# Attention with a softplus feed-forward on one core: low query parts turned by a DMA, their shifts by TensorE and small DMAs, and a planner with other DMA lags

## The chip, the cores and the metric

One core of a Trainium2 chip runs one launch of the kernel. The metric is device time in microseconds (us), lower is better. An execution is timed as a whole; one execution was also profiled.

## The reference

```python
q_pool = q.reshape(B, H, S // 2, 2, D).mean(axis=3)          # B 4, H 8, S 1152, D 64
scores = 1 / sqrt(D) * q_pool @ k.transpose(0, 1, 3, 2)
scores = scores - scores.max(axis=-1, keepdims=True)
attn = exp(scores) / (exp(scores).sum(axis=-1, keepdims=True) + 1e-9)
x = (attn @ v).transpose(0, 2, 1, 3).reshape(B * 576, H * D) # 2304 x 512
h = x @ w_in                                                 # w_in 512 x 2048
out = softplus(h) @ w_out                                    # w_out 2048 x 512
```

Neighbouring queries are averaged in pairs, so 576 query rows meet 1152 keys. q, k, v and w_in are drawn eight times larger than usual, so scores are large and the row maximum is needed to high precision.

## The kernel before

**Units of work.** The 32 heads go in 16 pairs (u0 to u15), two heads on one set of tiles. Attention of a pair is 18 steps: 9 key tiles for the first 256 query columns, then 9 for the other 320. Batches give 8 feed-forward blocks (U0 to U7, w_in and softplus; D0 to D7, w_out), which `ORDER` (L445) weaves between later pairs.

**Precision.** An fp32 operand is split into two fp16 parts, high and low, scaled by a power of two. Keys become `kcat` (high beside low) and queries `qcat` (high twice); both are turned into `kT` and `qA`, by TensorE for pair 0 and by a DMA transpose for the others (L736, L763). Scores are one matmul of `kT` with `qA` and a second one of `kB` (high keys plus two rows of a constant) with `qB`. `qB` holds the low queries (64 rows) and two rows of shift, the negated row maximum as a high and a low fp16 number.

**Preparing a pair** (`prepare`, L629). Load k and q, add neighbouring queries (L685), sums of squares on ScalarE (L686, L687), one matmul that adds both over partitions and a chain of small VectorE operations that makes both scales at once (`scale_from_squares`, L369), then the splits. The low queries go to `qlow` (L756).

**The maxima** (`maxima`, L797). For each of the 9 query tiles, TensorE scores high queries against key differences `kD` and keys, ScalarE takes the relu of one (L818), VectorE joins them and keeps the maximum (L822), and L838 does so for the last keys. A reduction (L857) and two small operations (L352, L355) put the shift as two more columns into `qlow`. TensorE turns `qlow`, low queries and shift together, against an identity (L879, L882: 20 matmuls for a pair), and ScalarE or VectorE copies the result to `qB` in three pieces (L896, L899).

**Attention** (`attention`, L930). Scores (L363), exp on ScalarE (L958), product with v (L967). The sums of exp are added up over key tiles by GpSimd or VectorE (`acc`, L435), and TensorE adds over partitions (L1038); for pairs in `SUMMED` (0, 2 and 4) TensorE does all of it (L983). Then a reciprocal by way of three small DMAs (L1054 to L1061) and a product.

**What sets the order.** `Sched` (L98) is a planner that runs while the program is built: each step has one or more engines it can go to, a price there, and a priority; tables `NUDGE` and `LEAN` shift priorities and prices. What it plans becomes the fixed order of instructions on each engine, and the engines then wait for each other by semaphores. DMAs are issued by one queue, SyncE's (SP), in the planned order. `LAG` (L103) is what it believes to pass from the end of a step to the start of one that depends on it; to a DMA 1,250 to 1,400 ns. Ring buffers (`raw` 4, `p` 4, `qlow` 2, PSUM `m` 3 and `s` 2) hold steps back.

Of the kernel before, what the change touches and what calls it, by code (L numbers as in the profile page):

```python
# [8 lines left out]
F32 = mybir.dt.float32  # L9
# [12 lines left out]
    "prep": [-1.5, 0, 3.75, 1, -3.25, 18.5, -0.75, 0, 0, -23.5, 26, 6.75, 0.25, 3, 6.75, 8.75],  # L22
    "value": [-7, 0, 6, -6.75, -3.25, 0, 4.75, -21.75, 10, -7.5, 5.25, -19, 0, -4.25, -8.75, -4.5],
    "most": [7.5, 3.75, 1, 0, -7.75, -2.25, 7.25, 9.25, 10, 9, 10.5, 0, 0, 21.75, 0, 0],
    "shift": [5.75, -3, -19.75, 17.75, -18.25, 12.5, -9.5, 0.5, -4, -19.75, 2.25, 2.25, 0, 1.25, 0, 8.5],
    "attend": [0.75, -2.25, -1, -8.5, 0, -34, -13.5, -10.25, 4.25, 0, 8.25, -4.5, 0, 6, 3, -2.25],
    "product": [-3.5, -0.5, 10, -6.25, 11.5, 9.25, 0, -1, 8, 24.75, 5.75, 1.75, 1, 6.5, 7.25, 0],
    "close": [12.5, -1.5, -29.5, -7.75, 14.75, -14.5, -4.25, 20.25, -13.5, -12, -1.25, 0, 0, 0.25, 14.75,
        -5.75],
    "win": [4.5, 9.5, 5.5, -20.25, 0, -9.75, -3.75, -48],  # L30
    "wout": [-0.5, -9, -18.5, 17.5, 39.25, -40.25, 12.25, 2.25, -1.5, -18.5, -11.25, -4.75, -1.25, 0, 26.25,
        4.75],
    "wparts": [0, -1, -7, 8.25, 3.75, -3.25, 42, -6.25, 19, -21, 0, -20.5, -17.5, -7.5, 2.5, 4.25],
    "split": [-26.75, -1.25, -1.75, 8.75, -4.75, 17.75, 1, 14],
    "up": [16.25, 1.5, 3, -3.25, 5.25, -23.25, -14.5, 2.75],
    "down": [1.75, -3, 37.25, -5.25, 4, -0.25, -4.25, 3.25],
# [16 lines left out]
        "split": [-100, -2200, 0, -1950, 1150, 0, 250, -200],
        "up": [1050, 400, -150, 0, 850, -100, -2300, 100],
        "down": [0, 0, 100, -1350, 50, 1800, -50, 650],
    },
    "ACT": {
        "prep": [500, 200, -3350, 0, -50, -750, -0, -1500, 250, 1300, 1850, -150, -800, 0, 0, 250],
        "value": [-350, 50, -1150, 150, 0, 0, -2050, 1000, -1200, -200, 400, 800, -650, 2750, -350, 900],
        "most": [100, -1400, 0, -0, -950, 100, 0, 0, -50, -1100, -350, 0, 600, -800, 0, 0],  # L60
        "shift": [-650, -400, 0, 100, -1400, -1350, -700, -900, 500, 2500, -4650, -900, -2150, 0, 900, 800],
        "attend": [1650, -1000, 2200, 500, -400, 1400, -250, 0, -100, 0, 350, 400, 0, 0, -0, 0],
        "product": [800, -1950, -2050, 3250, 900, 150, 1400, -3850, 2450, 1700, 1700, 100, 1100, 400, -150,
            1550],
        "close": [-450, -500, -1900, -900, -100, 1250, 0, 150, 800, 150, 0, 450, -1750, -1350, 750, 1250],
        "win": [950, -3550, -550, 100, 0, 300, -1750, -650],
        "wout": [300, 900, -750, -350, -550, 0, -1650, 50, 50, 150, 2900, 1050, -400, -700, 0, 100],
        "wparts": [1500, -250, 50, 0, 3300, 350, 3450, 2400, -400, -500, -1900, 0, 0, -400, 2600, 250],
        "split": [100, 0, -2250, -600, -1050, -400, -250, -200],
        "up": [-600, 2400, 50, 1500, -1750, 650, 600, 0],  # L70
        "down": [0, -2150, -900, 3150, 100, -900, 400, 900],
# [26 lines left out]
class Sched:  # L98

    LAG = {  # L103
        "PE": {"DVE": 200.0, "ACT": 200.0, "PE": 0.0, "DMA": 1300.0},
        "DVE": {"DVE": 40.0, "ACT": 45.0, "POOL": 60.0, "PE": 55.0, "DMA": 1400.0},
        "ACT": {"DVE": 45.0, "ACT": 40.0, "POOL": 60.0, "PE": 55.0, "DMA": 1250.0},
        "POOL": {"DVE": 50.0, "ACT": 60.0, "POOL": 50.0, "PE": 60.0, "DMA": 1300.0},
# [142 lines left out]
def pool1(n):  # L250
    return 145.0 + n * 0.95
# [1008 lines left out]
```

## Time and profile before

| what | value |
|---|---|
| time, median of 3 runs (lowest, highest) | 853.09 us (852.1, 857.29) |
| the profiled execution | 852.98 us |
| its span, first to last instruction | 851.3 us |
| TensorE busy, share of the span | 804.3 us, 94% |
| VectorE, ScalarE, GpSimd busy | 539.0, 492.8, 317.5 us |
| mean granted TensorE clock | 0.989 |

The trace's engines are PE (TensorE matmuls), PEld (its weight loads), DVE (VectorE), ACT (ScalarE), POOL (GpSimd) and SP (the queue that issues DMAs). A matmul's busy time has its pipeline in it, so a busy PE can still wait inside.

### The profile page before, as it was taken

Reading aid. Unit: us, or ns where it says so; the run is one execution under the profiler, and the core shown is the slowest. Engines: PE = TensorE matmul, PEld = TensorE weight load, DVE = VectorE, ACT = ScalarE, POOL = GpSimd, SP = SyncE. Lnnn points to the kernel's source line nnn. Section 1 sums busy time; section 2 is a strip of 40 time slices with the busy share of each in tenths; the row PEclk is TensorE's granted clock in tenths of the full one; section 3 lists DMA queues with packets and bytes.
Section 4 is the critical chain, followed back from the end, with each engine's and each line's share of the span. In section 5 each row is a group of like instructions: output and inputs, shape, how many; then the busy total and the mean of one; then the engine's idle time right before and its main releaser. Section 6 shows DMA issues by size and latency. Waiting matters only on the chain.

```text
span 851.3 us, 24268 instructions
## 1 busy us (share of the span) xinstructions
PE 804.3 (94%) x10250; PEld 579.0 (68%) x10250; DVE 539.0 (63%) x1171; ACT 492.8 (58%) x823; POOL 317.5 (37%) x272
## 2 busy tenths in 40 slices
PE   3898898989899999999999999999999999999997
PEld 2465566558767688768666787667876678775754
DVE  7778888889998876675685643466556626012520
ACT  4788899889897427562665545457865572120210
POOL 0105418521249201331676514611268882090000
PEclk9899999999999999999999999999999999999999
DMA  8718657358664710411652330420603000000000
GB/s 306 163 36 215 146 169 203 114 127 186 173 134 139 120 54 2 125 28 46 125 78 79 90 79 13 83 89 19 94 13 92 22 15 10 22 15 25 2 14 25
DMA packets 98093, 74.23 MB, mean 87 GB/s; under 512 B 64960, under 2 KB 79296, under 8 KB 97984
## 3 DMA queue, kind: packets, MB, share of 16 engines
q1 hardware_dynamic: 97984, 72.68, 34.6%
q8 instruction: 80, 1.31, 0.7%
q14 instruction: 29, 0.24, 0.1%
HBM read 49.81 MB, written 4.79 MB: 64 GB/s over the span
## 4 chain that ended last, share of the span: by engine, by line
PE 69%; DVE 11%; ACT 6%; DMA 5%; POOL 5%; issue 3%; SPq 1%; ACTq 0%; DVEq 0%; POOLq 0%
PE s L363 30%; PE m L363 26%; PE pv L967 12%; POOL acc L435 3%; DMA kT<-kcat 2%; ACT p L958 2%; PE pv L983 2%; DMA raw<-in_k_dram 1%; ACT raw L523 1%; DVE w L355 1%; DVE qlow L355 1%; DVE kcat L355 1%; DVE g L822 1%; PE m L1038 1%; DVE acc L435 1%
## 5 line engine op out<-in xcount | busy, mean ns | idle before, releaser
L958 ACT ACTIVATE p<-s,cols 128x512 f32<-128x512 f32 (+1 forms) x288 | 208.3, 741 | 79.1 <-PE s L363 44.0
L435 POOL TENSOR_TENSOR acc<-acc,p 128x512 f32<-128x512 f32 (+1 forms) x122 | 183.9, 1507 | 119.3 <-ACT p L958 78.1
L967 PE MATMUL pv<-p,v 128*64 128x320 f32 (+1 forms) x1152 | 189.6, 416 | 1.3 <-ACT rinv L1046 0.8
L363 PE MATMUL m<-w,gh 128*64 128x512 f16 x1152 | 175.9, 379 | 0.1
L363 PE MATMUL s<-qA,kT 128*64 128x320 f16 (+1 forms) x1152 | 159.0, 289 | 6.0 <-ACT p L958 5.5
L363 PE MATMUL s<-qB,kB 66*64 66x320 f16 (+1 forms) x1152 | 159.5, 289 | 0.0
L822 DVE CUSTOM_DVE_ANT_0 g<-m,g 128x512 f32<-128x512 f32 x144 | 98.1, 686 | 67.4 <-ACT g L818 37.4
L1199 ACT ACTIVATE g<-s,blk 128x512 f32<-128x512 f32 (+1 forms) x80 | 51.3, 642 | 148.5 <-PE s L363 113.4
L363 PEld LDWEIGHTS <-w1h 128*64 128x64 f16 x2048 | 117.6, 110 | 14.8 <-issue 1.6
L363 PE MATMUL m<-w,gl 128*64 128x512 f16 x576 | 113.5, 379 | 0.0
L363 PEld LDWEIGHTS <-gh 128*64 128x64 f16 x1152 | 71.3, 110 | 46.7 <-issue 0.7
L363 PEld LDWEIGHTS <-kT 128*64 128x64 f16 x1152 | 80.1, 111 | 31.9 <-issue 12.9
L818 ACT ACTIVATE g<-m 128x512 f32<-128x512 f32 x144 | 84.8, 596 | 26.7 <-PE m L363 22.5
L967 PEld LDWEIGHTS pv<-p,v 128*64 128x64 f32 x1152 | 77.7, 138 | 30.5 <-issue 11.2
L363 PEld LDWEIGHTS <-kB 66*64 66x64 f16 x1152 | 75.2, 111 | 19.9 <-issue 5.4
L363 PE MATMUL s<-xh,w1h 128*64 128x256 f16 (+1 forms) x1024 | 85.6, 286 | 0.3 <-ACT g L1199 0.2
L363 PE MATMUL s<-xh,w1l 128*64 128x256 f16 (+1 forms) x1024 | 85.5, 286 | 0.0
L363 PE MATMUL s<-xl,w1h 128*64 128x256 f16 (+1 forms) x1024 | 85.5, 286 | 0.0
L363 PEld LDWEIGHTS <-qA 128*64 128x64 f16 x864 | 52.6, 112 | 38.3 <-issue 20.7
L363 PE MATMUL m<-kT,qA 128*64 128x128 f16 (+1 forms) x576 | 74.7, 310 | 3.9 <-ACT g L818 2.0
L363 PE MATMUL m<-kD,qA 128*64 128x512 f16 x288 | 60.0, 397 | 5.6 <-DVE nm L822 3.4
L363 PEld LDWEIGHTS <-w1l 128*64 128x64 f16 x1024 | 59.8, 110 | 4.3
(147 smaller groups left out, 960.8 us busy)
## 6 DMA issues: line engine op xcount, KB each, us to landing
raw<-in_k_dram SPq DMA_DIRECT2D x16, 576.0 KB
v<-in_v_dram SPq DMA_DIRECT2D x16, 576.0 KB
raw<-in_q_dram SPq DMA_DIRECT2D x64, 128.0 KB
raw<-in_moe_w_out_dram SPq DMA_DIRECT2D x16, 512.0 KB
kB<-kT SPq DMA_DIRECT2D x32, 144.0 KB
gh<-in_moe_w_in_dram SPq DMA_DIRECT2D x4, 1024.0 KB
gl<-in_moe_w_in_dram SPq DMA_DIRECT2D x4, 1024.0 KB
out_dram<-g SPq DMA_DIRECT2D x16, 256.0 KB
```

Of the source, the lines that this page charges most:

```text
L355: nc.vector.scalar_tensor_tensor(out=out_, in0=in0, scalar=s, in1=in1, op0=op0, op1=op1)
L363: nc.tensor.matmul(out=out_[c:e], lhsT=lhsT[:, c:e], rhs=rhs, start=start, stop=stop, tile_position=(0, at + c))
L435: e.tensor_tensor(out=o, in0=a, in1=b, op=op)
L523: nc.scalar.activation(out=o, in_=i, func=ACTF.Square, accum_out=am)
L818: r = task([("ACT", act(512, 1), lambda: nc.scalar.activation(out=rest.item, in_=more.item, func=ACTF.Relu))], [y], prio, take=[rest], giv ...
L822: parts.append(task([("DVE", dve(512, 1.0, 1), lambda: nc.vector.tensor_tensor_reduce(out=rest.item, in0=most.item, in1=rest.item, scale=1 ...
L958: nc.scalar.activation(out=pt.item[:, :, 0:n], in_=s.item[:, :, 0:n], func=ACTF.Exp, scale=x.sc)
L967: nc.tensor.matmul(out=pv.item[h * 64:(h + 1) * 64, 0:n], lhsT=x.v.item[:, h, kt], rhs=pt.item[:, h, 0:n], start=(kt == 0), stop=(kt == KT ...
L983: nc.tensor.matmul(out=pv.item[g:g + 32, 512 - n // 2:512], lhsT=ones[:, 0:32], rhs=pt.item[:, h, a * n // 2:(a + 1) * n // 2], start=Fals ...
L1038: nc.tensor.matmul(out=ps.item[g:g + 32, 512 - n // 2:512], lhsT=ones[:, 0:32], rhs=acc.item[:, h, a * n // 2:(a + 1) * n // 2], start=Tru ...
L1199: x = task([("ACT", act(N, 1, 1), lambda: nc.scalar.activation(out=gs.item[:, 0:N], in_=ps.item[:, 0, 0:N], func=ACTF.Softplus, scale=ih[: ...
```

## The change

Three parts are visible in the code. The low queries of pairs 2 to 15 are no longer turned by TensorE: a DMA transpose writes them to `qB`, the shifts alone are written into a tile `sh`, turned by one small product, copied to `row`, and moved to rows 64 and 65 of `qB` by small DMAs. Pair 0 makes its key scale and its query scale apart. And the planner has other numbers: the lag from a step to a DMA falls from about 1,300 ns to 60 to 150 ns, prices are altered, a shared port of GpSimd and VectorE is charged for more operations, and both tables are new. Beside that, `SUMMED` names pairs 0 to 3, two rows of pair 0 take their maximum over whole rows (`PLAIN`), loads of w_in and of later pairs wait for pair 0's `kB`, the squares of v are written to a `p` buffer instead of a `raw` one, `qlow` has one buffer, and exps and scores are held in turn.

```diff
-    "wout": [-0.5, -9, -18.5, 17.5, 39.25, -40.25, 12.25, 2.25, -1.5, -18.5, -11.25, -4.75, -1.25, 0, 26.25,
+    "wout": [-4.5, 7.25, -1.5, -13, -1.75, -2.75, -10, 4.75, 25.75, 17, 23, 1.75, -96.75, 26, -6.5, 0],
...
-        "PE": {"DVE": 200.0, "ACT": 200.0, "PE": 0.0, "DMA": 1300.0},
-        "DVE": {"DVE": 40.0, "ACT": 45.0, "POOL": 60.0, "PE": 55.0, "DMA": 1400.0},
+        "PE": {"DVE": 200.0, "ACT": 200.0, "PE": 0.0, "DMA": 150.0},
+        "DVE": {"DVE": 40.0, "ACT": 45.0, "POOL": 60.0, "PE": 55.0, "DMA": 60.0},
...
-    SUMMED = (0, 2, 4)
+    SUMMED = (0, 1, 2, 3)
+    TURNED = (0, 1)
+    PLAIN = {0:(1,5)}
...
-        both = scale_from_squares(
-            cols[:, u, 0:2], cols[:, u, 2:4], cols[:, u, 4:6], cols[:, u, 6:8], [y, z], prio)
+        if u == 0:
+            both = scale_from_squares(c[0], c[2], c[4], c[6], [z], prio)
+            q_scale = scale_from_squares(c[1], c[3], c[5], c[7], [y], prio)
...
+        if u not in TURNED:
+            y = task([("DMA", 1445.0, lambda: nc.sync.dma_start_transpose(
+                out=blk(x.qB), in_=x.qlow.item.rearrange("p t d -> p (t d)")), 640.0, -500.0)], [x.ql_done], prio + 3.0,
+                take=[x.qB], give=[x.qlow])
...
+                y = small(lambda ts_=ts_, hs=hs: ts(x.sh.item[:, hs], x.nm.item[:, ts_], 1.0 / SHIFT, ALU.mult),
+                          [y], prio, take=[] if half else [x.sh], port=True)
...
+                    nc.tensor.matmul(out=ps.item[0:64, 0:128], lhsT=x.sh.item[:, 32 * half:32 * half + 64], rhs=ident,
+                                     start=True, stop=True, tile_position=(0, 0))
...
+                def move(half=half, row=row, first=first, last=last, nt=nt, o=32 * half):
+                    nc.sync.dma_start(out=blk(x.qB)[D:D + 2, first:last], in_=row.item[o:o + 2 * nt])
+                    if half:
+                        m = o + MIX - first
+                        nc.sync.dma_start(out=x.qB.item[D:D + 2, T * 128:T * 128 + 64], in_=row.item[m:m + nt + 1:nt, 64:128])
...
-        jk = Hold(raw_r)
+        jk = Hold(p_r)
```

How the order moves is shown at three places. The first is VectorE at the start of the program, pair 0 (`raw_72` holds its keys, `raw_73` its queries, `cols` the scales). Before:

```order
L435 TENSOR_TENSOR raw_73<-raw_73 128x9x64
L352 TENSOR_SCALAR cols<-m_108 128x2
L352 TENSOR_SCALAR cols<-cols 128x2 x2
L380 RECIPROCAL cols<-cols 128x2
L352 TENSOR_SCALAR cols<-cols 128x1
L352 TENSOR_SCALAR kcat_78<-raw_72,cols 128x9x64
L352 TENSOR_SCALAR qcat_84<-raw_73,cols 128x1152
L355 SCALAR_TENSOR_TENSOR kcat_78<-raw_72,cols,kcat_78 128x9x64 x2
```

and in the changed kernel:

```order
L352 TENSOR_SCALAR cols<-m_109 128x1
L352 TENSOR_SCALAR cols<-cols 128x1 x2
L385 RECIPROCAL cols<-cols 128x1
L352 TENSOR_SCALAR kcat_78<-raw_72,cols 128x9x64
L440 TENSOR_TENSOR raw_73<-raw_73 128x9x64
L355 SCALAR_TENSOR_TENSOR kcat_78<-raw_72,cols,kcat_78 128x9x64 x2
L352 TENSOR_SCALAR cols<-m_111 128x1
L352 TENSOR_SCALAR cols<-cols 128x1 x2
L385 RECIPROCAL cols<-cols 128x1
```

The key scale and both key splits now stand around the query sum and ahead of the query scale, and the 1152-wide query split has left VectorE for ScalarE.

The second is ScalarE where the first piece of a pair's `qB` is copied. Before, for pair 4, from the copy (`qB_89`) to the pair's first exp (`p_93`, the first of width 2x256):

```order
L896 ACTIVATE qB_89<-m_110 66x2x256
L958 ACTIVATE p_92<-s_105,cols 128x640
L818 ACTIVATE g_101<-m_109 128x512
L818 ACTIVATE g_102<-m_108 128x512
L958 ACTIVATE p_93<-s_106,cols 128x2x256
```

and in the changed kernel for pair 3, from the copy of its first shifts (`row_87`) on, the pair's first exp being fifteen rows behind it:

```order
L946 ACTIVATE row_87<-m_109 8x128
L846 ACTIVATE g_105<-m_111 128x512
L1048 ACTIVATE p_92<-s_107,cols 128x640
L530 ACTIVATE gh,amw<-raw_74 128x1024
L1048 ACTIVATE p_94<-s_106,cols 128x640
L407 ACTIVATE kcat_78<-raw_72,cols 128x9x64 x2
L407 ACTIVATE qcat_84<-raw_73,cols 128x1152
L1048 ACTIVATE p_95<-s_107,cols 128x640
L846 ACTIVATE g_102<-m_110 128x512
```

One exp of the pair ahead stood between the copy and the pair's own exps; now there are three, with a k split, a q split and squares among them.

The third is SP's queue in the changed kernel, from a load for w_out to the next loads, where pair 2's shifts are moved (`row_87` to `qB_90`) and pair 3's low queries are turned (`qlow_85` to `qB_91`):

```order
L593 DMA raw_73<-in_moe_w_out_dram 128x1024
L593 DMA raw_72<-in_moe_w_out_dram 128x1024
L954 DMA qB_90<-row_87 2x4x128
L593 DMA raw_74<-in_moe_w_out_dram 128x1024
L1150 DMA scratch<-few_100 128x4
L751 DMA_TRANSPOSE kT_80<-kcat_78 128x18x128
L779 DMA_TRANSPOSE qA_89<-qcat_84 128x9x128
L1153 DMA rinv_98<-scratch 128x1x256
L789 DMA_TRANSPOSE qB_91<-qlow_85 128x9x128
L663 DMA raw_72<-in_k_dram 128x2x576
L758 DMA kB_83<-kT_80 64x1152 x2
L954 DMA qB_90<-row_87 2x5x128
```

The queue before has `kT`, `qA` and `kB` for a pair, with neither the transpose of `qlow` nor the moves of `row`; the three moves and one transpose of a pair now stand among loads, transposes and the small DMAs of the sums, 56 more DMAs in all.

## Rows read from the trace of the kernel before

**Rows 1.** The page: busy share of each engine in 40 equal slices, in tenths.
```profile
PE   3898898989899999999999999999999999999997
...
DVE  7778888889998876675685643466556626012520
ACT  4788899889897427562665545457865572120210
```

**Rows 2.** Stretches: us, then busy us of each engine, clock, DMA share, GB/s.
```profile
0.00:32.30 32.30, 15.59 (x126) 8.32 (x128) 25.76 (x55) 18.50 (x32) 3.33 (x10) 0.91 0.93 269
32.30:250.00 217.70, 200.18 (x2711) 140.40 (x2709) 187.53 (x419) 189.82 (x334) 75.35 (x61) 0.97 0.57 150
250.00:852.00 602.00, 588.49 (x7420) 430.28 (x7417) 325.66 (x700) 284.49 (x458) 238.80 (x202) 1.00 0.24 55
```

**Rows 3.** PE's waits by releaser: us in total, times, longest.
```profile
PE m L363 <- ACT qcat L523: 11.0, 2, 8.9
...
PE m L363 <- DVE nm L822: 5.1, 6, 1.8
PE m L363 <- DVE qlow L355: 3.7, 5, 1.3
```

**Rows 4.** Timeline of the start: start us, us, engine line operation [idle before <-releaser].
```profile
5.92 0.19 ACT L523 ACTIVATION_READ_ACCUMULATOR kcat<-raw 128x1 f32 x1
...
7.32 0.76 DVE L435 TENSOR_TENSOR raw<-raw 128x576 f32<-128x576 f32 x1 [1.36 <-DMA raw<-in_q_dram]
...
8.94 0.38 PE L363 MATMUL m<-cols,ones 128*64 128x2 f32 x4 [8.94 <-ACT qcat L523]
...
10.23 0.81 DVE L352 TENSOR_SCALAR kcat<-raw,cols 128x576 f16<-128x576 f32 x1
...
12.28 1.53 DVE L355 SCALAR_TENSOR_TENSOR kcat<-raw,cols,kcat 128x576 f16<-128x576 f32 x2
...
17.04 0.64 PE L363 MATMUL m<-kD,qA 128*64 128x512 f16 x2 [0.21 <-DVE kT L728]
```

**Rows 5.** Groups of PE: count | busy us, mean ns | idle before.
```profile
L363 PE MATMUL m<-ident,qlow 128*64 128x128 f16 x256 | 15.8, 224 | 6.9 <-DVE qlow L355 3.7 <-DVE nm L838 1.0 <-DVE blk L1084 0.8
L983 PE MATMUL pv<-p,ones 128*32 128x160 f32 x216 | 11.0, 318 | 0.0
```

**Rows 6.** Groups of ACT by form, same columns.
```profile
L896 ACT ACTIVATE qB<-m 66x320 f16<-66x320 f32 x18 | 7.1, 427 | 5.7 <-PE m L363 5.6
...
L896 ACT ACTIVATE qB<-m 66x512 f16<-66x512 f32 x10 | 5.8, 584 | 2.1 <-PE m L363 2.1
...
L1046 ACT ACTIVATE rinv<-m 128x128 f32<-128x128 f32 x4 | 1.1, 274 | 0.1
```

**Rows 7.** Instructions on the tile qlow: ns min/median/max.
```profile
L352 DVE TENSOR_SCALAR qlow<-nm x32: 158/176/1265, 27.3 to 680.1; 128x4 f16<-128x4 f32 x16, 128x5 f16<-128x5 f32 x16
L355 DVE SCALAR_TENSOR_TENSOR qlow<-nm,qlow x32: 164/178/1537, 28.4 to 680.3; 128x4 f16<-128x4 f32 x16, 128x5 f16<-128x5 f32 x16
```

**Rows 8.** Timeline around pair 4's first shifts and scores.
```profile
152.12 9.38 POOL L435 TENSOR_TENSOR acc<-acc,p 128x640 f32<-128x640 f32 x5
...
155.18 1.09 DVE L355 SCALAR_TENSOR_TENSOR qlow<-nm,qlow 128x4 f16<-128x4 f32 x1
...
156.33 0.41 PE L363 MATMUL m<-ident,qlow 128*64 128x128 f16 x7 [0.80 <-DVE blk L1084]
...
158.14 0.33 PE L363 MATMUL s<-qB,kB 66*64 66x256 f16 x2
```

**Rows 9.** Timeline: two DMAs in a row of one sum.
```profile
723.32 0.32 SPq L1058 DMA_DIRECT2D scratch<-few  x1
...
725.58 0.52 SPq L1061 DMA_DIRECT2D rinv<-scratch  x1
```

**Rows 10.** The chain that ended last: start us, us, what.
```profile
64.82 4.25 DMA qA<-qcat
...
815.37 31.09 PE m L363 x288
```

More of the change, by code (lines that the diff above doesn't have):

```diff
@@ L222, in run @@
                         else:
[L223 removed]
+                            wire = max(max(now + 390.0, wire) + tag, done - 20.0)
                         done = wire + self.LANDS
@@ L364, in tiled, with blk, small @@
                              tile_position=(0, at + c))
-    def small(fn, deps, prio, n=1, take=(), give=()):
-        return task([("DVE", 165.0 + 20.0 * (n > 1), fn)], deps, prio, take=take, give=give)
+    def blk(h):
+        t = h.item
+        return t if len(t.shape) == 3 else t[:, 0:T * 128].rearrange("p (a b) -> p a b", b=128)
+    def small(fn, deps, prio, n=1, take=(), give=(), port=False):
+        way = ("DVE", 165.0 + 20.0 * (n > 1), fn)
+        return task([way + ("port",) if port else way], deps, prio, take=take, give=give)
     def scale_from_squares(am, t, s, inv, deps, prio):
@@ L412, in hi_ways @@
         ways = {"ACT": (act(n, ap=1), on_act), "POOL": (pool1(n), on_pool, "port"),
-                "DVE": (dve(n, 1.0 if n == 576 else 1.7), on_dve, "port")}
+                "DVE": (dve(n, 1.0) + 50.0 if n in (576, 1152) else dve(n, 1.7) + 30.0, on_dve, "port")}
         return [(e, *ways[e]) for e in engines]
@@ L439, in load @@
     def load(fn, queue, wire, deps, prio, take):
-        return task([("DMA", queue, fn, wire)], deps, prio, take=take)
+        return task([("DMA", queue + 95.0, fn, wire)], deps, prio, take=take)
     ORDER = ("u0", "u1", "u2", "u3",
@@ L523, in on_act @@
             nc.scalar.activation(out=o, in_=i, func=ACTF.Square, accum_out=am)
-        return task([("ACT", act(n), on_act)], [dep], prio, take=take, give=give)
+        return task([("ACT", 105.0 + (act(n) if n in (576, 1152) else 212.0 + n * 0.924), on_act)], [dep], prio,
+                    take=take, give=give)
     def staged(n):
@@ L868, in maxima, with low_rows, turn_shift, views @@
         x.qB_done = [[], []]
+        def low_rows(out_, c, rhs, start, stop):
+            for lo in (0, STRIP):
+                nc.tensor.matmul(out=out_[lo:lo + STRIP], lhsT=x.low()[:, c, 2 - lo // 32:D + 2 - lo // 32], rhs=rhs,
+                                 start=start, stop=stop, tile_position=(0, lo))
+        if x.u not in TURNED:
+            for half in range(2):
+                prio = x.was + x.early * 7.2 * (half + 1) + 0.2
+                first, last = ((0, 4), (4, T))[half]
+                nt = last - first
+                ps, row = Hold(m_r), Hold(row_r)
+                def turn_shift(half=half, ps=ps):
+                    nc.tensor.matmul(out=ps.item[0:64, 0:128], lhsT=x.sh.item[:, 32 * half:32 * half + 64], rhs=ident,
+                                     start=True, stop=True, tile_position=(0, 0))
+                y = task([("PE", pe(1, 128) + 10.0, turn_shift)], [half_done[half]], prio, take=[ps], give=[x.sh])
+                def views(ps=ps, row=row, nt=nt, o=32 * half):
+                    return row.item[o:o + 2 * nt], ps.item[o:o + 2 * nt, 0:128]
+                def on_act(views=views):
+                    o, i = views()
+                    nc.scalar.activation(out=o, in_=i, func=ACTF.Copy)
+                def on_dve(views=views):
+                    nc.vector.tensor_copy(*views())
+                y = task([("ACT", act(128, 1), on_act), ("DVE", dve(128), on_dve)], [y], prio, take=[row], give=[ps])
+                def move(half=half, row=row, first=first, last=last, nt=nt, o=32 * half):
[3 more added lines that the diff above has]
+                        nc.sync.dma_start(out=x.qB.item[D:D + 2, T * 128:T * 128 + 64], in_=row.item[m:m + nt + 1:nt, 64:128])
+                x.qB_done[half] = [*x.qB_low, task([("DMA", 645.0 * (1 + half), move, 30.0 * (1 + half))], [y, *x.qB_low], prio, give=[row])]
+            return
         for half, h in ((0, None), (1, 0), (1, 1)):
@@ L1225, in tile_attention_softplus_ffn @@
                                 pattern=[[-1, 128]], channel_multiplier=1)
+        for some in sh_r.free:
+            nc.vector.memset(some, 0.0)
+        for some in qlow_r.free:
+            nc.gpsimd.memset(some[:, :, 64:128], 0.0)
         for kb in kB_r.free:
             nc.vector.memset(kb[D:D + 2], SHIFT)
-        if ROWS > D + 2:
-            for low in qlow_r.free:
-                nc.gpsimd.memset(low[:, T * (D + 2):], 0.0)
         sd.run()
```

257 lines of the change are left out of this document (144 added, 113 removed).

## The prediction

> **What bounds the kernel now.** I read the page's slices first [rows 1]. TensorE is near full from the seventh slice on, and VectorE and ScalarE are full only in the first twelve. So the run has two parts, and I cut it by stretches [rows 2], at 32.30 us, where the first scores with `qB` begin, and at 250 us. From 250 us on PE is busy 588.49 of 602.00 us at a clock of 1.00: that part is bound by PE's own work, and only 13.5 us of it are idle. Before 250 us PE is idle 16.7 us of the first 32.30 and 17.5 us of the next 217.70. In that second stretch ACT is busy 189.82 us (87%), DVE 187.53 us (86%), and the granted clock is 0.97, so some time went by at 1.2 GHz. No engine there is full; three engines near their limit wait for each other, and the order of work decides.
>
> Then the waits [rows 3]. PE waits 11.0 us for the query squares, nearly all of it the 8.94 us before the first matmul [rows 4], and 5.1 and 3.7 us for VectorE's maxima and for the shift that it writes into `qlow`. These are the waits that the change touches. PE's busy time hides more. 288 matmuls of 512 columns take 31.09 us where nothing disturbs them [rows 10], 0.108 us each; by columns all matmuls of the program would need about 743 us (an estimate from this pace and the counts), so some 100 us of the span are lost, most of them before 250 us.
>
> **The change part by part.** The sum is made against the profiled execution, 852.98 us (span 851.3 and 1.7 around it), which is 0.1 under the median 853.09.
>
> *Start of pair 0: -3 us.* The key squares are read out by 6.11 us (5.92 and 0.19), but the joint matmul starts at 8.94, after the query squares. From there to the key split is 1.29 us (10.23 less 8.94), and the last key split ends at 13.81 (12.28 and 1.53) [rows 4]. With a scale of its own the key split can start at about 7.4; behind it VectorE now has one split of 0.81, the query sum of 0.76 and two splits of 1.53, so the keys are ready near 10.5, 3.3 us earlier. The query scale comes behind these and its wide split is on ACT, so the query transposes stay near 12.5; they no longer have the keys behind them. The first maxima matmul, at 17.04, should come at about 14. Bounds: nothing, if the maxima wait for something else anyway, and -5.
>
> *Turns of the shift: -4 us.* The 20 matmuls of a pair go for 14 pairs, two of 128 columns come in. The 256 wide ones took 15.8 us busy, 1.0 us a pair [rows 5]; by pace (0.027 us for 128 columns) all 20 are 0.49 us and the two new ones 0.05. So a pair saves 0.4 to 1.0 us. I take the pace, because these matmuls mostly stand in a full stream, and count only pairs 7 to 15, which lie in the stretch that PE bounds: 9 times 0.43. Bounds -4 and -9.
>
> *Copies to `qB`: -2 us.* ACT needed 12.9 us for 28 of them (7.1 and 5.8), 0.46 each, three a pair: 1.4 us. Two copies of 128 columns are nearest to 0.274 each [rows 6], plus one 64-wide copy of low queries, which I take at 0.2 as an estimate from the same row. That is 0.6 us a pair off ACT and DVE. Pairs 2 to 6 are prepared while these engines are near full: 3 us over two engines. Bounds 0 and -4.
>
> *Sums on TensorE: 0.* `SUMMED` has four pairs for three. The wide half of the sums took 11.0 us for three pairs [rows 5], so a further pair costs PE up to 7 us busy. It is added in pairs 1 and 3, where ACT is nearer its limit than PE; pair 4 loses its own. If the cover is gone, +7. On the other side 16 fewer adds remain, and the order gives GpSimd 87 of them where it had 136; of its 272 instructions 198 are left.
>
> *Waits around the shift, and GpSimd beside VectorE: -5 us.* The two small operations that write a shift take 0.176 and 0.178 us at the median and up to 1.265 and 1.537 [rows 7]. Pair 4 shows it: five adds of GpSimd fill 9.38 us from 152.12, one of the small operations takes 1.09 us at 155.18, PE's turn waits until 156.33, and the scores start at 158.14, right behind the copy [rows 8]. PE's two waits of this kind are 8.8 us in all [rows 3]. The new order does two things here. It takes 49 adds from GpSimd, and it sets the turn of a shift ahead: by counting columns in the order, 1.4, 1.8, 2.9 and 1.6 us of matmuls stood between the first turn and the first scores of pairs 3, 4, 5 and 15, and now at least 6.7 for every pair from 2 on, and at least 5.1 for second halves (the order of ACT shows the same, three exps where there was one). I take a little over half of the 8.8. Bounds 0 and -9.
>
> The Trainium skill, "SBUF — State Buffer", says of the port pair that VectorE and GpSimd share that it is locked for a whole instruction and the loser fully blocks; the 1.09 us beside adds of 1.88 us agrees. By that rule the delay goes only where GpSimd is silent, in pairs 1 to 3, and comes back with the adds of pair 4, and this term would be nearer -3, the sum 839.
>
> *Work set ahead: -2 us.* By the same count 3.1 us more matmul work stands ahead of pair 6's first scores than before, most of it from U0. If the stretch before 250 us takes no longer for it, it is off the part that PE bounds. Bounds 0 and -3.
>
> *New DMAs: 0.* A shift now goes turn, copy, DMA, scores. One small DMA is followed by one that needs its landing after 2.26 us (723.32 to 725.58) [rows 9]. With a copy of 0.27 and a turn of 0.41 that is 3.0 us, where turn and copy alone were 1.0. The 5.1 to 6.7 us of matmuls between cover it; without the cover, 2 us for each of 28 halves. The 14 transposes of `qlow` have the shape of `qA`'s, whose landing held the chain for 4.25 us in the early stretch [rows 10], where the DMA engines are 57% busy [rows 2]. They start as soon as low queries exist, well ahead of use. I take 0, with +20 as the upper end (five early pairs times 4.25).
>
> Sum: -3 -4 -2 +0 -5 -2 +0 = -16, so 852.98 - 16 = 837.0 us. The ends added up are 823 and about 880, which do not meet at once.
>
> **The rivals.**
>
> *The early part gains more.* For it: PE is idle 17.5 us between 32 and 250 us and was at a lower clock in part, and the whole order was made anew with other lags. Against it: ACT is 87% busy there, and its work up to pair 6 hardly falls. If half of that idle time goes beside the terms above, another 9 us go: 828 us.
>
> *The order brings nothing.* A new order can be as good as the old one on the chip; every engine still waits for whichever step is late. Then only removed work counts: half of the start and the turns, -5.5, 847.5 us. For it: ACT's near-full stretch. Against it: the waits at pairs 3, 4, 5 and 15 are named in the trace, and the distance there has grown.
>
> *The moves of the shift hold the scores: slower.* The mechanism is the one queue. In the new order of SP a move can stand behind transposes; two of them at 4.25 us each [rows 10] and the chain of 3.0 us make 11.5 us, against 6.7 us of cover: 4.8 us lost. It decides once SP holds a move by more than 3.7 us. If six pairs meet that, +29 -16, 866 us. For it: 56 more DMAs in a queue in which every DMA waits for those ahead, and in the order shown the second move of pair 2 stands behind three transposes. Against it: its first move stands ahead of them, and by the same count pair 2's second half has 9.3 us of cover. The Trainium skill, "DMA: Bandwidth & Descriptors" (Specifications), adds that transfers under 512 bytes are done by read-modify-write, and the rows moved here are 256 bytes; no run here shows its price.
>
> **How the numbers follow.** The forecast has 0.46, the larger gain 0.25, no gain from the order 0.17, the slower case 0.12. About 1% (8.5 us) is what a measurement can tell from no change. The first two are faster by more than that, 0.71; the third lies within it, 0.17; the last is slower, 0.12. The range runs from 820, below the larger gain with some room, to 857, past the third case and some way to the slower one; it leaves out most of that one and a tail below.
>
> **What would show it.** Right: first scores near 29 us; PE idle before 250 us clearly under the 34.2 us of now; PE's waits for `nm` and for the shift under half; the small shift operations near 0.18 us in pairs 1 to 3; no wait of a score matmul for a DMA into `qB`. Wrong: scores that wait for `qB` from `row`, a landing of `kT` or `qA` held up by the transposes of `qlow`, ACT waiting longer for `p` buffers, or a stretch from 32 to pair 6's scores that is no shorter than now although the start is.

## The result, and the profile after

The kernel after takes 822.42 us (median of 4 runs, 822.01 to 829.45), the kernel before in the same comparison 854.32 us. The ratio is 0.9644, 95% interval 0.9583 to 0.9705: faster. The forecast was 837.0 in a range of 820 to 857, so the sign and the range hold. The profiled execution took 822.01 us, 31.0 less than the 852.98 of before, where the sum gave 16 less. The time is nearest to the rival "the early part gains more" (828), and 5.6 us below it.

The page's slices of the kernel after, to be laid beside [rows 1]:

```profile
PE   4899999999999999999999999999999999999997
...
DVE  7978989896987867575623664675473742012310
ACT  6899899996966667656657675656565762232620
```

The stretches of the kernel after, with the cuts of [rows 2]:

```profile
0.00:32.30 32.30, 18.40 (x212) 10.92 (x214) 28.05 (x68) 23.69 (x40) 1.97 (x8) 1.00 0.83 245
32.30:250.00 217.70, 211.34 (x2904) 146.14 (x2902) 191.72 (x468) 192.50 (x340) 40.03 (x41) 1.00 0.68 158
250.00:852.00 602.00, 562.94 (x7020) 413.38 (x7016) 278.18 (x650) 310.89 (x494) 163.83 (x149) 1.00 0.26 60
```

From the third slice to the last but one PE shows 9; in [rows 1] six of the first eleven show 8. In the middle stretch its idle time is 217.70 less 211.34, 6.4 us, where it was 17.5, and the clock is 1.00, where it was 0.97. The two helpers are fuller than before (88% each), GpSimd is half as busy (40.03 for 75.35 us). The third row ends 31.7 us behind the span's end; up to there PE is idle 7.4 us.

PE's waits by releaser in the kernel after, as in [rows 3]:

```profile
PE m L363 <- ACT kcat L530: 6.1, 1, 6.1
PE s L363 <- ACT p L1048: 3.8, 6, 1.4
...
PE m L363 <- DVE nm L850: 1.9, 5, 0.8
...
PE m L363 <- DMA qA<-qcat: 1.0, 2, 0.6
```

The wait for the query squares is gone: the first matmul waits 6.1 us for the key squares alone. The wait for the shift is gone too, and the one for the maxima is 1.9 for 5.1 us. No matmul waits for a DMA into `qB`.

The start of the kernel after, timeline as in [rows 4]; the last line is the first score matmul with `qB`, at 32.3 us before:

```profile
5.90 0.19 ACT L530 ACTIVATION_READ_ACCUMULATOR kcat<-raw 128x1 f32 x1
...
6.14 0.38 PE L363 MATMUL m<-cols,ones 128*64 128x1 f32 x4 [6.14 <-ACT kcat L530]
...
7.34 0.81 DVE L352 TENSOR_SCALAR kcat<-raw,cols 128x576 f16<-128x576 f32 x1
...
8.73 1.54 DVE L355 SCALAR_TENSOR_TENSOR kcat<-raw,cols,kcat 128x576 f16<-128x576 f32 x2
...
14.57 0.64 PE L363 MATMUL m<-kD,qA 128*64 128x512 f16 x2 [0.69 <-DVE qA L743]
...
24.89 0.30 PE L363 MATMUL s<-qB,kB 66*64 66x256 f16 x2
```

**Where the time went.** A view of my own shows the place: every matmul is counted by its columns at the pace of [rows 10], in order of start, and the table gives when so much work had been done. The fp32 products with v count 1.88 times their columns; with that all of it is 743.5 us before and 741.4 after. By bare columns it would be 682.0 and 679.9.

| work done, us | 5 | 25 | 50 | 100 | 125 | 200 | 400 | 725 |
|---|---|---|---|---|---|---|---|---|
| before, at us | 29.6 | 55.1 | 88.3 | 153.8 | 190.1 | 276.5 | 488.9 | 827.5 |
| after, at us | 22.7 | 50.7 | 81.6 | 143.8 | 171.0 | 252.0 | 462.4 | 798.8 |
| difference | -6.9 | -4.4 | -6.7 | -10.0 | -19.1 | -24.5 | -26.5 | -28.7 |

Of 31 us, 24.5 are won by the point where 200 us of work are done, 4.2 behind it, and 2.1 are work that is no longer there. So it is mostly the early part, up to pair 6. What the other engines did up to that point, by stretches of before (to 276.50) and of after (to 252.00):

```profile
0.00:276.50 276.50, 240.98 (x3180) 167.70 (x3182) 237.62 (x515) 227.82 (x399) 102.85 (x88) 0.97 0.62 162
```

```profile
0.00:252.00 252.00, 231.74 (x3136) 158.32 (x3138) 221.77 (x537) 217.86 (x381) 41.99 (x49) 1.00 0.70 170
```

For the same TensorE work VectorE has 15.9 us less, ScalarE 10.0 and GpSimd 60.9. Not all of that is work that went away. The page's totals after:

```profile
PE 792.7 (97%) x10130; PEld 570.4 (70%) x10130; DVE 497.9 (61%) x1183; ACT 527.1 (64%) x872; POOL 205.8 (25%) x198
```

Over the whole program ScalarE is busy 34.3 us longer than before, VectorE 41.1 us shorter. So ScalarE's early relief is no saving: behind 250 us it has more to do (310.9 us for 284.5), in a part where it has time.

VectorE's instructions up to that point are more (537 for 515) and yet take less. The small operations of the shift show a part of it, in groups by form of the middle stretch, before (`qlow`) and after (`sh`).

```profile
L355 DVE SCALAR_TENSOR_TENSOR qlow<-nm,qlow 128x4 f16<-128x4 f32 x6 | 3.2, 533 | 0.1
...
L352 DVE TENSOR_SCALAR qlow<-nm 128x4 f16<-128x4 f32 x6 | 2.2, 372 | 0.1
```

```profile
L355 DVE SCALAR_TENSOR_TENSOR sh<-nm,sh 128x4 f16<-128x4 f32 x5 | 1.4, 280 | 0.0
...
L352 DVE TENSOR_SCALAR sh<-nm 128x4 f16<-128x4 f32 x5 | 1.1, 214 | 0.0
```

The four columns take 0.21 to 0.28 us in the mean where they took 0.37 to 0.53. The same stretch by tile (ns min/median/max) shows that most of them are as short before as after:

```profile
L355 DVE SCALAR_TENSOR_TENSOR qlow<-nm,qlow x12: 164/178/1411, 34.7 to 227.9; 128x5 f16<-128x5 f32 x6, 128x4 f16<-128x4 f32 x6
```

```profile
L355 DVE SCALAR_TENSOR_TENSOR sh<-nm,sh x10: 150/161/770, 81.0 to 233.8; 128x4 f16<-128x4 f32 x5, 128x5 f16<-128x5 f32 x5
```

A few are held and make the mean: of both operations and both widths, 7 of 24 before (0.63 to 1.41 us each) and 2 of 20 after (0.43 and 0.77).

### The profile page after: what moved, and what is told of

It reads as the page before. It is cut to its first block, busy times and chain, and to the rows that moved or that the text cites. A ratio compares the mean times of both kernels' runs of the same rounds, so it can differ in the third digit from the quotient of the medians.

```text
span 820.3 us, 24090 instructions
## 1 busy us (share of the span) xinstructions
PE 792.7 (97%) x10130; PEld 570.4 (70%) x10130; DVE 497.9 (61%) x1183; ACT 527.1 (64%) x872; POOL 205.8 (25%) x198
## 4 chain that ended last, share of the span: by engine, by line
PE 72%; DMA 9%; DVE 8%; ACT 4%; issue 2%; SPq 2%; POOL 1%; DVEq 0%; ACTq 0%; POOLq 0%
PE s L363 31%; PE m L363 27%; PE pv L1059 13%; DMA qA<-qcat 2%; DMA rinv<-scratch 2%; DVE acc L440 1%; DMA v<-in_v_dram 1%; PE pv L1075 1%; DMA raw<-in_k_dram 1%; DVE g L850 1%; DVE w L355 1%; DMA raw<-in_q_dram 1%; DMA raw<-in_moe_w_out_dram 1%; ACT p L1048 1%; PE m L1130 1%
## 5 line engine op out<-in xcount | busy, mean ns | idle before, releaser
L1048 ACT ACTIVATE p<-s,cols 128x512 f32<-128x512 f32 (+1 forms) x288 | 211.2, 744 | 63.0 <-PE s L363 41.8
L1059 PE MATMUL pv<-p,v 128*64 128x320 f32 (+1 forms) x1152 | 185.4, 411 | 0.0
L440 POOL TENSOR_TENSOR acc<-acc,p 128x512 f32<-128x512 f32 (+1 forms) x77 | 108.9, 1414 | 105.7 <-ACT p L1048 59.7
L355 DVE SCALAR_TENSOR_TENSOR gl<-g,blk,gh 128x512 f16<-128x512 f32 (+1 forms) x72 | 50.4, 702 | 95.0 <-ACT gh L407 91.1
L440 DVE TENSOR_TENSOR acc<-acc,p 128x640 f32<-128x640 f32 (+1 forms) x91 | 74.2, 815 | 15.6 <-ACT p L1048 14.6
L363 PE MATMUL m<-kT,qA 128*64 128x512 f16 (+1 forms) x572 | 69.4, 300 | 1.9 <-DVE nm L850 0.7
```

Source lines behind the costliest of these rows:

```text
L355: nc.vector.scalar_tensor_tensor(out=out_, in0=in0, scalar=s, in1=in1, op0=op0, op1=op1)
L363: nc.tensor.matmul(out=out_[c:e], lhsT=lhsT[:, c:e], rhs=rhs, start=start, stop=stop, tile_position=(0, at + c))
L440: e.tensor_tensor(out=o, in0=a, in1=b, op=op)
L1048: nc.scalar.activation(out=pt.item[:, :, 0:n], in_=s.item[:, :, 0:n], func=ACTF.Exp, scale=x.sc)
L1059: nc.tensor.matmul(out=pv.item[h * 64:(h + 1) * 64, 0:n], lhsT=x.v.item[:, h, kt], rhs=pt.item[:, h, 0:n], start=(kt == 0), stop=(kt == KT ...
```

## The experiments

Twelve kernels. Times are medians; the kernel before ran beside each group of four, at 854.1, 854.8 and 854.6 us. E1 to E3 and E9 keep the order of the kernel after exactly and make one part dearer; E4 does so with before. The others have a new order from the planner.

**E1: the shift's products nine times.** Does TensorE's work count?

```diff
-                    nc.tensor.matmul(out=ps.item[0:64, 0:128], lhsT=x.sh.item[:, 32 * half:32 * half + 64], rhs=ident,
+                    for _ in range(9):
+                        nc.tensor.matmul(out=ps.item[0:64, 0:128], lhsT=x.sh.item[:, 32 * half:32 * half + 64],
```

> The changed kernel with its order of work kept, and each of the 28 products that turn a shift issued nine times into the same columns: 224 matmuls of 128 columns come back, one after the other, some 0.053 us each by pace, 12 us of TensorE work in all, about 7 of it for pairs 7 to 15. Theory 'removed matmul work is time' (the term of -4 us for the turns): 5 to 10 us slower than the changed kernel, 828 to 832. Rival 'the turns stood in waits and cost nothing': within 2 us of 822.

830.30 us (829.5 to 831.9), ratio 0.9736 [0.9710, 0.9761]: 7.9 us more. In its trace the nine products of a turn start 0.055 to 0.056 us apart, so the 224 added ones are 12.5 us of TensorE; 63% of that came out as time. In this order TensorE's work counts, so the term "turns" was rightly priced as work in a nearly full stream.

**E2: the copies of the shift's rows four times.** Does work on ScalarE and VectorE count?

```diff
-                    nc.scalar.activation(out=o, in_=i, func=ACTF.Copy)
+                    for _ in range(4):
+                        nc.scalar.activation(out=o, in_=i, func=ACTF.Copy)
...
-                    nc.vector.tensor_copy(*views())
+                    for _ in range(4):
+                        nc.vector.tensor_copy(*views())
```

> The changed kernel with its order kept, and each copy of a turned shift done four times: 84 copies of 128 columns at about 0.27 us more on ScalarE and VectorE, some 23 us, a little more than the copies to qB that the change took away. Theory 'these engines set the early part' (the term of -2 us): 2 to 5 us slower, 824 to 827. Rival 'their idle time takes it': within 1 us of 822.

836.64 us (834.2 to 839.2), ratio 0.9809 [0.9778, 0.9839]: 14.2 us more, and both theories are missed. The tile `row` in its trace, then in the kernel after:

```profile
L951 DVE CAST row<-m x68: 268/279/284, 95.7 to 668.1; 8x128 f16<-8x128 f32 x36, 10x128 f16<-10x128 f32 x32
L947 ACT ACTIVATE row<-m x44: 249/267/269, 83.3 to 656.8; 10x128 f16<-10x128 f32 x24, 8x128 f16<-8x128 f32 x20
```

```profile
L949 DVE CAST row<-m x17: 268/279/284, 94.5 to 652.5; 8x128 f16<-8x128 f32 x9, 10x128 f16<-10x128 f32 x8
L946 ACT ACTIVATE row<-m x11: 250/268/268, 82.7 to 641.8; 10x128 f16<-10x128 f32 x6, 8x128 f16<-8x128 f32 x5
```

84 copies more at some 0.27 us are 23 us on the two helpers, and 14.2 of them came out, 8.5 of these before 200 us of work. So a microsecond added at the shift cost 0.6 us in the mean, far more than I had thought of engines that PE outlasts. It is no even price. Only 30 of the 84 copies, 8 us, stand before 200 us of work; and from 100 to 125 us of work, where one copy of a shift became four (0.8 us more), the loss grows from 1.8 to 6.8 us. The later 5.7 us fall where both helpers have time to spare. Each longer copy also makes its shift later, and the run doesn't part that from the engines' load.

**E3: each move of a shift issued twice.** How thin is the cover of the new DMAs?

```diff
-                    nc.sync.dma_start(out=blk(x.qB)[D:D + 2, first:last], in_=row.item[o:o + 2 * nt])
+                    for _ in range(2):
+                        nc.sync.dma_start(out=blk(x.qB)[D:D + 2, first:last], in_=row.item[o:o + 2 * nt])
```

> The changed kernel with its order kept, and each move of a pair's shifts issued twice: 28 more DMAs, so each shift lands about 0.7 us later and all that SP issues behind it too. Theory 'the matmuls set between a shift and its scores cover the move': within 2 us of 822. Rival 'the moves hold the scores': 28 times 0.7, 10 to 20 us slower, 832 to 842.

835.45 us (834.6 to 836.6), ratio 0.9795 [0.9769, 0.9820]: 13.0 us more. Waits of the issuing queue in its trace:

```profile
SPq L955 <- DMA qB<-row: 54.7, 28, 6.3
```

The second issue writes the same rows and waits for the first to land: 28 waits, 2 us each. So the run shows what it costs when this queue stands still for 2 us at a shift. PE's waits of its middle stretch say who pays:

```profile
PE m L363 <- DMA qA<-qcat: 2.4, 2, 2.3
PE s L363 <- ACT g L1292: 2.4, 3, 1.9
PE m L363 <- DVE nm L850: 2.3, 3, 1.1
...
PE s L363 <- DMA qB<-row: 1.1, 1, 1.1
```

Only 1.1 us is the scores' own wait. PE waits 2.4 us for a transpose of queries (0.6 in the kernel after), and ScalarE 8.7 us for loads of w_out (3.9), so what stands behind the held queue pays. 2.6 us are lost by 75 us of work and nearly all of it by 150. The ground of the slower rival, one queue for all DMAs, is real, then; its own form, scores that wait for a move, cost 1.1 us here and nothing in the kernel after.

**E4: the kernel before with idle matmuls for the clock.** 30 products of the identity ahead of the small sums of pairs 1 to 5 and of the weights.

```diff
+            for _ in range(warm):
+                nc.tensor.matmul(out=ps.item[0:64, 0:128], lhsT=ident[:, 0:64], rhs=ident, start=True, stop=True,
+                                 tile_position=(0, 0))
             tiled(ps.item[:, 0:am.shape[-1]], ones, am, True, True)
```

> The kernel before, its order kept, with 30 matmuls of the identity ahead of the small sums over partitions of pairs 1 to 5 and of the w_in parts, where TensorE waits; they are written over by the sums. They take about 1.6 us each of 13 places where TensorE does not wait. Theory 'the clock of 1.2 GHz in four stretches before 250 us is part of what the change got back': granted clock above 0.993 and 2 to 6 us faster than before, 847 to 851. Rival 'the clock fell because the other engines were late, and costs nothing by itself': clock higher or not, time the same or up to 10 us slower for the added work, 853 to 863.

865.91 us, ratio 1.0152 [1.0125, 1.0178]. Its stretches:

```profile
0.00:32.30 32.30, 13.70 (x132) 8.23 (x134) 23.30 (x49) 16.19 (x28) 3.02 (x10) 0.93 0.83 253
32.30:250.00 217.70, 205.55 (x2950) 154.12 (x2952) 178.59 (x397) 180.48 (x319) 71.18 (x58) 0.99 0.54 145
```

By the clock record of its trace, the kernel before fell to 1.2 GHz at 71.0, 105.1 and 180.2 us of its middle stretch. The stretches of before that end there:

```profile
64.80:71.00 6.20, 3.59 (x54) 2.16 (x52) 4.41 (x11) 4.96 (x11) 2.68 (x2) 1.00 1.18 232
98.00:105.10 7.10, 4.20 (x64) 2.35 (x59) 5.26 (x12) 5.91 (x11) 2.53 (x2) 1.00 0.93 246
173.00:180.20 7.20, 5.55 (x80) 3.51 (x68) 7.20 (x12) 5.62 (x10) 3.31 (x2) 1.00 0.82 203
```

PE was short of work ahead of each. In E4 none of the three falls is left, the stretch has 0.99 for 0.97, and 11.8 us were lost all the same. That is above the range of both theories and a little more than the 10.5 us by columns that the idle matmuls add. So the clock's return in the kernel after looks like a mark of the gain and not a cause of it; a gain that is small beside the 10.5 us could not be seen here.

**E5 to E7: without the fitted tables.** E5 is the kernel after and E6 the kernel before with all entries of `NUDGE` and `LEAN` at zero:

```diff
+for _t in (NUDGE, *LEAN.values()):
+    for _k in _t:
+        _t[_k] = [0.0] * len(_t[_k])
```

E7 is E6 with the lags of the kernel after:

```diff
-        "PE": {"DVE": 200.0, "ACT": 200.0, "PE": 0.0, "DMA": 1300.0},
+        "PE": {"DVE": 200.0, "ACT": 200.0, "PE": 0.0, "DMA": 150.0},
...
-    HEAD = {"DVE": 195.0, "POOL": 330.0}
+    HEAD = {"DVE": 140.0, "POOL": 140.0}
```

> The kernel after with all entries of its two tables set to zero, so that the order comes from the planner's costs and lags alone; parts and instructions are those of the kernel after. If the fitted tables carry the gain, this loses 20 us or more against the 822.4 of the kernel after and ends near the tableless kernel before (next run), within 10 us of it. If the parts carry the gain (fewer turns, lighter copies, fewer adds on GpSimd, two small scales at the start), both tableless kernels lose alike and this one stays about 30 us under the tableless kernel before.

> The kernel before with its two tables set to zero. The partner of the run above. If the tables carry the gain: within 10 us of the tableless kernel after. If the parts carry it: about 30 us above that one. By itself it should lose 5 to 30 us against the 854 of the kernel before.

> The kernel before with tables at zero, as in the run above, and the planner's lags of the kernel after (a task behind a DMA is thought ready 50 to 150 ns after it is done and not 1250 to 1400, the head of VectorE and GpSimd 140 ns). The parts are those of before. If the true lags make the better order, this is 10 us or more under the tableless kernel before; if the lags only matter together with the parts or the tables, the two lie within 5 us.

E5 took 841.72 us, ratio 0.9855 [0.9821, 0.9890]; E6 910.80, 1.0660 [1.0631, 1.0689]; E7 901.12, 1.0548 [1.0524, 1.0572]. The tables are worth 19.3 us after and 56 before; the lags 9.7 us by themselves. But most of the distance from E7 to E5 is one accident, the timeline of PE in E6 before the first feed-forward block:

```profile
211.96 0.69 PE L368 MATMUL m<-g,ones 128*64 128x128 f32 x4 [8.03 <-POOL g L390]
219.10 0.38 PE L368 MATMUL m<-amw,ones 128*64 128x1 f32 x4 [6.44 <-ACT gl L528]
222.12 0.38 PE L368 MATMUL m<-amw,ones 128*64 128x1 f32 x4 [2.64 <-ACT gh L528]
```

PE stands for the scales of the weights, with nothing planned in between; between 125 and 150 us of work E6 falls from 4.8 to 65.5 us behind the kernel before. From 190 to 285 us its PE waits some 50 us in all, and the granted clock is 1.2 GHz for 54.6 us of these 95, so the slow clock comes on top of the waits. Up to 125 us of work, ahead of the accident, E5 is 12.6 us earlier than E6 and 17.8 earlier than E7, and 11.2 later than the kernel after. From E6 to the kernel after that is 23.9 us, and 12.6 of them need no table: parts, prices and lags together bring about half of this distance, the fitted order the other half. Up to there the lags alone bring nothing, for E7 is behind E6. E6 and E7 can't be read for more.

**E8: all pairs turned by TensorE, with the tables.** `TURNED = tuple(range(16))`, in place of `(0, 1)`.

> The kernel after with its tables and lags, but the low queries of all 16 pairs turned by TensorE with their shift, as pairs 0 and 1 are (18 to 20 small matmuls and two wide copies a pair again, no transpose of low queries and no small DMA of the shift); the planner makes a new order for it. By pace TensorE's added work is 14 times 0.44 us, 6 us. If the turned parts carry the gain, this gives back 15 to 25 us (837 to 847). If the order carries it, it costs its 6 us and what an unfitted order costs, about 8 to 12 (830 to 835). Under 828 would say that the new way of moving the shift is worth little.

842.70 us (841.3 to 844.6), ratio 0.9869 [0.9843, 0.9896], 20.3 us more. That is about what the tables were worth in E5 (19.3), so it doesn't tell the part from a table that no longer fits; E11 looks at the part without tables.

**E9: GpSimd kept busy, order as after.** Pairs 1 to 5, 30 row maxima:

```diff
+                if 1 <= x.u <= 5 and c % 3:
+                    spare = xm[1].rearrange("p a b -> p (a b)")
+                    nc.gpsimd.tensor_scalar(out=spare[:, 0:8], in0=ident[:, 0:8], scalar1=x.nm3.item[:, c, 0:1],
+                                            scalar2=0.0, op0=ALU.mult, op1=ALU.add)
+                    for _ in range(2):
+                        nc.gpsimd.tensor_tensor(out=spare, in0=spare, in1=spare, op=ALU.add)
```

> The kernel after in its own order, with idle work for GpSimd in the early stretch: behind 30 of the row maxima of pairs 1 to 5 GpSimd writes eight columns scaled by that maximum and then adds a tile of 256 columns to itself twice (nobody reads the result). That is some 60 us of GpSimd time, as much as the kernel before had more of it up to the same point of TensorE's work (102.9 us against 42.0). If adds on GpSimd lengthen what VectorE does beside them, and this was a good part of the early gain, the kernel loses 5 to 12 us before 250 us, and the shift's small operations grow from 0.2 us towards the 0.4 to 0.5 of before. If that neighbourhood is worth little, it loses under 3 us. A loss with waits for GpSimd itself (the copies beside qA and qB) would say nothing on either.

837.78 us (835.9 to 838.5), ratio 0.9797 [0.9774, 0.9821]: 15.4 us more, above what was expected. The loss is complete at 150 us of work (17.3 there, 8.1 at 125). Groups of its middle stretch, and its stretch up to 200 us of work:

```profile
L851 DVE CUSTOM_DVE_ANT_0 g<-m,g 128x512 f32<-128x512 f32 x54 | 36.5, 682 | 8.5 <-ACT g L846 7.0 <-ACT p L1057 0.9 <-PE m L363 0.2
...
L355 DVE SCALAR_TENSOR_TENSOR sh<-nm,sh 128x4 f16<-128x4 f32 x5 | 2.5, 492 | 0.0
...
L352 DVE TENSOR_SCALAR sh<-nm 128x4 f16<-128x4 f32 x5 | 1.4, 282 | 0.0
```

```profile
0.00:268.70 268.70, 235.03 (x3136) 160.79 (x3138) 227.14 (x537) 219.07 (x381) 97.40 (x140) 0.99 0.64 159
```

The 537 instructions of VectorE are the same as in the kernel after to 252.00, and take 5.4 us more. The maxima, which read PSUM, stay at 682 ns (683 after). The shift's operations on four columns grow in the mean, to 0.49 and 0.28 us, near the 0.53 and 0.37 of before: up to 250 us, 5 of 19 are held for 0.57 to 1.22 us (three TENSOR_SCALAR, two SCALAR_TENSOR_TENSOR), and the others take 0.14 to 0.17. The Trainium skill, "SBUF — State Buffer" (SBUF: two separate sides), says that VectorE contends with GpSimd only in its faster two-port modes or with two inputs in SBUF. The maxima and the two held SCALAR_TENSOR_TENSOR agree with it; a TENSOR_SCALAR of the shift has one input, and whether it ran in such a mode no run here shows.

By subtraction some 10 us are left for waits. One of PE's in the middle stretch, which the kernel after doesn't have there:

```profile
PE m L945 <- DVE sh L355: 5.0, 3, 3.9
```

The timeline at pair 5's second shift:

```profile
189.26 1.53 POOL L440 TENSOR_TENSOR acc<-acc,p 128x640 f32<-128x640 f32 x1
...
190.83 2.00 DVE L440 TENSOR_TENSOR acc<-acc,p 128x640 f32<-128x640 f32 x1 [4.49 <-POOL acc L440]
...
192.75 0.16 DVE L352 TENSOR_SCALAR sh<-nm 128x5 f16<-128x5 f32 x1
...
193.43 0.15 DVE L355 SCALAR_TENSOR_TENSOR sh<-nm,sh 128x5 f16<-128x5 f32 x1
...
193.63 0.24 PE L945 MATMUL m<-ident,sh 128*64 128x128 f16 x1 [3.95 <-DVE sh L355]
```

GpSimd comes late to an add; VectorE, next in the same sum, waits 4.49 us for it; the shift stands behind that add, and PE waits 3.95 us for the shift. This is GpSimd's own lateness, of which the expectation said that it would blur the test, so the 15.4 us are not the price of the neighbourhood alone, and the run doesn't part the two. What it does show is two ways by which GpSimd's load in the early part becomes time.

**E10 to E12: one part undone in E5, without tables.** So that no order is fitted to either: E10 finds pair 0's scales together again, E11 turns all pairs, E12 has the sums of before.

```diff
-        if u == 0:
+        if u < 0:
```

```diff
-    TURNED = (0, 1)
+    TURNED = tuple(range(16))
```

```diff
-    SUMMED = (0, 1, 2, 3)
+    SUMMED = (0, 2, 4)
```

> The kernel after without tables (as the run at 841.7), and the scales of pair 0 found together again as before. If the separate scale's lead stays to the end, this is 3 to 7 us slower than 841.7; if the first stretch's lead is eaten by what follows (the work curve of the kernel after lost 2.5 of 6.9 us by 25 us of work), 0 to 3; a faster run would say that two plans without tables differ by more than this part is worth.

> The kernel after without tables, with the low queries of all pairs turned by TensorE again. Against the 841.7 without tables and the 842.7 of the turned kernel with its tables. If the new way of the shift is worth its parts (TensorE 6 us by pace, copies 0.6 us a pair at near-full engines), this is 8 to 20 us slower than 841.7 (850 to 862). If the 20 us that the turned kernel lost with its tables were the tables' misfit, it is within 6 us of 841.7.

> The kernel after without tables, with pairs 0, 2 and 4 summed on TensorE as before, in place of pairs 0 to 3. If the early sums on TensorE (and the GpSimd adds that go with them) carry the early gain, this is 4 to 12 us slower than 841.7; if pair 1 and 3 lose nothing by it, it lies within 3 us.

E10 took 840.09 us, ratio 0.9828 [0.9802, 0.9854]; E11 841.60, 0.9845 [0.9817, 0.9873]; both as E5. E12 took 849.85, 0.9943 [0.9917, 0.9968], 8.1 us more than E5, with intervals that don't meet, although TensorE has 3.9 us less work by columns. In the profiled executions, 12.1 us apart, it falls behind E5 early: 5.6 us at 50 us of work, 13.5 at 125. The sums on tile `acc`, E12 and then E5, to 252 us:

```profile
L445 DVE TENSOR_TENSOR acc<-acc,p x23: 675/811/826, 66.7 to 251.7; 128x640 f32<-128x640 f32 x15, 128x512 f32<-128x512 f32 x8
L445 POOL TENSOR_TENSOR acc<-acc,p x18: 1267/1320/2276, 70.5 to 246.3; 128x512 f32<-128x512 f32 x13, 128x640 f32<-128x640 f32 x5
```

```profile
L445 DVE TENSOR_TENSOR acc<-acc,p x21: 676/804/1961, 169.5 to 251.7; 128x512 f32<-128x512 f32 x11, 128x640 f32<-128x640 f32 x10
L445 POOL TENSOR_TENSOR acc<-acc,p x10: 1266/1412/2522, 171.3 to 237.3; 128x512 f32<-128x512 f32 x6, 128x640 f32<-128x640 f32 x4
```

With pairs 0 to 3 summed on TensorE these adds begin at 169.5 us (at 159.2 in the kernel after); with 0, 2 and 4 at 66.7, in the middle of the stretch in which VectorE and ScalarE are near full. Each of E10 to E12 has an order of its own; that E10 and E11 came out within 1.6 us of E5 speaks against a new order as the cause of 8.1 us, but three runs don't exclude it.

## Why the prediction came out as it did

The range held and the sum did not: it gave 16 us where 31 were won. The time lies 2.4 us above the range's lower end, within the room that was left below the larger-gain rival; that it fell inside is no merit of the terms.

*What bounds the kernel.* Right: two parts, and the early one, in which the order and three engines near full decide, holds most of what could be won. Its 743 us of matmul work "by columns" is no count of bare columns, which gives 682; so the 100 us that it calls lost hang on what fp32 products are taken to cost. The ends of its terms add up to 876, not to about 880.

*Start, -3.* The steps came as worked out: key split at 7.34 (about 7.4 said), first maxima matmul at 14.57 (about 14). The first scores stand at 24.89, better than the 29 of the list of marks; by work done the lead is 6.9 us at first and 4.4 at 25 us of work. The term was a little small in this order. In the order without tables the part is worth nothing that could be measured (E10).

*Turns, -4.* Right in kind (E1) and near in size where it was counted: from 200 us of work to 725, 4.2 us are won. That is the whole late part, not the turns alone, so the near match is in part luck. Without tables, turns and copies undone together cost nothing (E11: 841.60 for 841.72).

*Copies, -2.* Near what E2's mean of 0.6 us for each us makes of 3 us. But no such price was put on the rest that left VectorE and ScalarE in the early part, 25.8 us in all by the stretches above. At 0.6 those 25.8 us would be some 15 us. This is an estimate and not shown: the price is uneven (E2), and a part of the 25.8 us is in the other terms.

*Sums on TensorE, 0.* **This is the step that failed, as far as the runs show one.** I weighed up to 7 us of PE's added work against cover on PE, and put the adds that go away early at nothing. E12 measures the part, in an order without tables: 8.1 us lost when pairs 1 and 3 go back to adds and pair 4 to TensorE. The early sums go from helpers that are near full to TensorE, which waits for them there, and pair 4's come back as adds, later. What it is worth in the fitted order was not measured; 8.1 would be about half of the miss.

*Waits around the shift and GpSimd, -5.* Right in the waits that it names: 8.8 us became 1.9, so 6.9. E9 shows two ways by which such waits come. The rule of the Trainium skill beside it ("SBUF — State Buffer", Terms: the loser of the shared port pair fully blocks) made the term -3, with the delay back from pair 4's adds on. After 159 us, where these begin, two of the shift's operations are held indeed (0.43 and 0.77 us), but PE's waits name no shift; so the rule's place came out, and its price did not.

*New DMAs, 0.* Right for the kernel after: no score waits for `qB`. E3 shows how thin the queue's slack is: 2 us of standstill at each shift, and 13 us are gone, though hardly by scores that wait for a move, as the slower rival had it.

*The rivals.* "The early part gains more" describes best what happened, and where: half of the 17.5 us of idle time was to go, and 11.1 went, with the clock 0.03 higher. The time is still 5.6 us under its 828. "The order brings nothing" falls: the tables alone are worth 19.3 us in the kernel after (E5). Still, 841.7 without tables beats the fitted kernel before by 13 us, so the gain is not the tables' alone.

The size of the miss, 15 us, is thus the early part: -12 forecast for it (start, copies, sums, waits, work ahead) and -24.5 measured.

*What stays open.* What each part is worth in the fitted order: parts undone there lose the fit as well (E8), and the parts tried without tables are not additive. The loads that now wait for the pair before, pair 0's two maxima by a plain reduction, the work that moved between helpers, and the planner's prices of single instructions were not tried by themselves. So what makes up the 12.5 us that the early part won beyond its terms is not measured in the order of the kernel after. None of the runs beats the kernel after.

## What to carry to other kernels

Where several engines are near full and wait for each other, don't put their work at nothing: a run with the same order and one part made dearer shows what it costs (here 0.6 us per us in the mean, very unevenly), and this goes for moves between engines too, not only for work that goes away. A kernel with a fitted order should be compared part by part without its fit, or with its order kept; undoing a part under the old tables cost 20 us here for a part that is worth nothing without them. And look at what stands behind a late helper on its customer's queue: an add that nobody hurries for held the shift, and through it the scores.

## What the runs showed of the hardware

- Products on one half of the array, one behind the other, start 0.056 us apart for 128 columns (E1), twice the 0.027 by which the prediction priced turns that alternate between halves. So the two new products of a pair are 0.11 us and not 0.05.
- Taking away the stretches at 1.2 GHz (three short ones) by idle matmuls gave no time back that could be seen: 11.8 us were lost for 10.5 us of added matmuls (E4).
- A small DMA that is made to wait until the one before it has landed holds the queue some 2 us (E3: 28 waits, 54.7 us).
- Beside GpSimd's added work VectorE's maxima of 512 columns stayed at 0.68 us (E9). The shift's small operations are either short or held: 0.14 to 0.17 us, or 0.4 to 1.2 us, 5 of 19 held with that work and 2 of 20 without it.
